# A written-out instruction order, replaced from about a sixth of the kernel onward

## The chip, the core and the metric

The kernel runs on one core of a Trainium2 chip. That core has five engines with instruction queues of their own: TensorE (PE in the profile, with PEld for its weight loads), VectorE (DVE), ScalarE (ACT), GpSimd (POOL) and SyncE (SP), which here only issues transfers. Each engine works through its queue strictly in order, and waits on semaphores where an instruction needs what another engine or a transfer has not yet delivered. The metric is the device time of one execution in microseconds; a smaller one is better.

## What is computed

Attention over 8 batches, 8 heads, 576 tokens and 64 dimensions a head, with 16 further "beacon" keys and values in front that every token may see, and then an ELU network over the 4608 tokens that result:

```python
scores = scale * q @ concat(beacon_k, k).T        # causal among the 576, beacons always seen
a = softmax(scores);  x = a @ concat(beacon_v, v) # per head; heads side by side: (4608, 512)
h = x @ w_in                                      # (4608, 2048)
g = where(h > 0, h, exp(min(h, 0)) - 1)
out = g @ w_out                                   # (4608, 512)
```

## The kernel before

**Attention.** Heads are taken in pairs: pair n is heads 2*(n%4) and 2*(n%4)+1 of batch n//4, 32 pairs in all. For batches 0 to 3 a pair's k and q are loaded (load_k, load_q), cast to bf16 (cast_pair, into one of three `sb` buffers), turned on PE (do_T) and copied out of PSUM (do_kT on DVE, do_qT on ACT or DVE). For batches 4 to 7 the loads are by token (load_tok, cast_tok) and the turning is done by transposing transfers on SP (turn_tok). The scores of a pair come in a few units SC (L568); ACT takes their exponential (L578, two instructions a unit, out of two PSUM banks into an `et` buffer), POOL zeroes what the causal mask hides (L583), PE multiplies by the values and a column of ones (AV, L597), and DVE divides (do_norm: L610 and L611). The result x is turned by PE or, from batch 2 on, by transposing transfers (turn_x, L617), into xT.

**The network.** It works on 11 tiles of tokens: two of 128, one of 256, then eight of 512 (tiles 3 to 10). In a tile of 512 the first matrix takes 16 steps of four matmuls (do_mm1, L649), each into one PSUM bank; here "step (p, i)" is step i of tile p. Each step's bank goes through three others: ACT takes exp into one of eight `wide` buffers (do_e, L656), a clamp to [0, 1] follows (do_clamp, L660), and DVE joins the two branches of ELU (do_join, L671), which frees the bank and the `wide` buffer and leaves half of a `gt` buffer. The second matrix of tiles 3 to 10 is done by the Strassen-Winograd scheme: seven products of half size (P1 to P7, do_PR, L725), each in two halves of eight matmuls, with DVE making four kinds of sums from the `gt` buffers (S3 L698, S1 L701, S2 L704, S4 L707). The sums of weights that it needs are made once (T1 to T4, tile `wt`); before that `wt` serves as further load buffers. Products leave PSUM by copies (do_Xcopy, ACT or DVE) and additions (do_Xadd, L735) into `wide` buffers, and those are written out by SP or ACT (do_put, L739). Tiles 0 to 2 use a plain second matrix (do_mm2, L767).

**What sets the order.** Nothing schedules at build time. All operations are first recorded with what they depend on and which buffers they take and give; each gets a number. Then Program.run walks three tables: ORDER (the numbers, in the order in which the operations are to be emitted, with -1 for a filler matmul), PICKS (a letter for every operation that more than one engine could do) and PLACES (which buffer of its kind each operation takes). Where two places of the list use the same buffer, the later one waits for the earlier. The lines that turn the tables into a program:

```python
for op in self.ops:
    if len(op.engines) > 1:
        op.eng = next(picks)
for i in order:
    ...
    for room in op.take:
        at = int(next(places), 36)
    ...
    op.fn(self.engines[op.eng], *got, *op.args)
```

An operation with a choice names its engines when it is recorded: the clamp is `add("GV", do_clamp, ...)`, so POOL or DVE; a cast of k and q is `"GA"`, POOL or ACT; a load or a put is `"SA"`, the queue of SP or of ACT. The join is DVE's alone, and exp is ACT's.

Of the kernel before, what the change touches and what calls it, by code (L numbers as in the profile page):

```python
# [29 lines left out]
301 251 254 261 278 302 320 958 279 303 280 282 288 304 281 1019 283 305 1020 309 306 311 959 284 308 340 1028  # L30
310 312 411 321 412 285 295 960 1065 322 323 428 1089 1033 1066 413 1067 1037 1090 512 1034 1035 1093 1038
1039 399 297 1094 1095 358 429 400 292 1057 1058 1059 1036 1049 1050 430 1051 409 324 1041 1091 1092 1042 1043
1040 1096 445 1068 462 446 307 414 1060 536 415 416 1081 1082 1083 410 359 1052 1097 290 1053 1054 463 313 417
431 432 433 1044 1029 1022 1023 1055 447 1024 434 341 342 1025 343 293 289 464 1056 344 1026 1084 1073 1074
1075 448 449 526 1085 1086 450 1076 407 465 1087 1045 1046 1047 1061 1062 314 1030 405 451 1063 466 1088 1048
1069 1070 1071 1072 408 1077 1078 1079 467 291 360 468 401 1064 649 978 979 1080 315 351 349 316 317 350 352
354 403 1098 980 981 1031 1101 1027 542 982 331 335 336 337 361 543 1102 362 332 334 1021 363 364 406 333 380
1099 381 1100 329 345 330 1105 508 1108 1106 371 365 346 1107 366 384 325 537 1109 1115 961 402 538 347 530
1104 372 531 983 385 506 374 368 375 326 328 353 1032 355 369 1103 1118 367 373 348 376 377 378 370 1112 544
379 327 1113 390 1120 382 392 1110 1111 1116 527 356 357 391 1121 383 520 539 540 541 386 387 521 522 1117 388  # L40
1126 1127 1142 393 395 389 397 418 479 480 481 1114 1128 1119 1124 419 1134 435 439 441 396 394 1135 1122 436
437 1130 404 1136 440 442 443 1125 424 444 425 514 1123 528 529 452 422 423 426 1131 427 515 504 453 454 1132
1152 1153 523 1160 484 510 485 458 475 476 1154 478 438 1161 1192 1193 1155 488 421 489 1156 1157 459 1162
1163 1158 1194 1195 627 505 524 532 1159 533 1184 1185 1186 1209 1168 1169 1170 1171 1176 1177 525 1138 1178
1148 1149 1144 1145 1150 1139 545 1187 1180 513 1181 1200 1201 643 644 1179 1146 1147 1151 1182 477 398 1183
1202 516 1137 1196 1197 1172 1198 1173 473 474 534 456 1164 1165 1174 460 1166 1208 617 1203 461 621 1204 1199
1188 517 518 457 622 1189 650 1190 469 1212 1175 1211 1167 492 496 1216 486 470 493 535 1141 455 1191 1213
1229 1217 1205 490 472 1210 1206 1207 1214 497 502 1215 1223 1224 1219 1220 420 482 471 494 501 487 1222 1221
500 495 483 1133 491 503 1218 1226 623 1227 1228 507 572 556 1231 573 628 1225 1230 1235 499 557 559 558 1237
637 638 576 552 498 553 550 551 1232 1241 577 1234 651 574 1233 1242 511 1243 519 645 1238 1239 1240 579 562  # L50
563 647 1252 560 586 1236 646 561 1263 1264 1271 1250 1287 587 578 1265 1266 1295 633 1272 1288 1299 1273 1274
1296 1297 1298 1300 1301 1267 1268 618 1245 509 593 740 652 554 629 630 1289 624 631 750 1269 594 1290 1251
648 1249 601 1270 1255 1256 588 1246 1247 565 1303 1304 602 1305 570 632 566 567 615 568 1311 1257 569 1302
1312 639 1313 555 1258 641 1253 1259 1260 1261 1291 1292 597 625 1306 1320 1275 640 1314 634 598 1262 1319 734
571 1276 591 582 546 1279 1293 1294 575 1283 583 580 564 584 592 635 756 547 548 599 1280 1281 581 1284 585
642 1277 1323 636 1278 600 595 1340 596 549 1324 589 613 603 590 606 1307 1315 1285 604 1282 1308 609 1327 607
608 1286 1316 1309 1317 1328 1310 1318 735 619 741 718 1331 611 1143 1329 673 674 679 659 660 680 1330 1341
1322 1326 1337 1334 1346 677 653 693 654 656 694 1321 1325 1335 678 1342 742 1332 1366 1367 863 751 682 757
1368 662 1248 616 728 1333 1345 1343 626 743 1344 661 736 1390 1338 1374 1375 620 758 744 745 1422 1378 1379
1391 1380 1392 1406 1369 1398 1399 737 1376 1377 1381 1400 1382 1393 1339 1431 681 1394 676 738 729 1370 1383  # L60
1363 1401 1423 1348 1424 1395 1396 1407 726 1426 722 1425 1371 1414 1140 752 1349 1408 847 754 1409 1386 1372
614 1384 1415 1416 1397 1360 1373 1336 1352 1353 1385 739 695 1417 1387 1388 1389 1354 655 1350 1427 612 730
1428 663 1361 1433 657 664 759 1402 1403 746 666 1404 1410 605 1411 1429 675 841 1405 665 706 1418 1419 1420
658 747 1244 731 707 748 732 749 1412 1413 1356 1357 1421 1358 753 669 683 670 1351 689 672 1430 1437 690 691
1451 696 704 697 1434 1438 1435 692 1364 1432 684 686 671 685 698 699 667 687 610 688 705 1436 1439 1444 668
1440 708 709 848 700 701 1129 1452 1456 702 710 703 790 766 791 767 711 733 713 714 827 857 724 1445 1446 1447
842 858 1457 864 865 755 1254 760 761 780 800 801 1441 1365 1453 1442 1454 1448 1443 1449 1450 792 723 1497
1498 802 1517 1455 1355 1347 781 1518 1519 1499 1481 1533 835 1493 1520 1494 1495 768 782 829 1482 725 1501
1534 849 1496 1500 851 1535 1536 852 866 717 1543 1459 720 836 1525 1526 1527 1528 1472 1485 1486 1487 1477
1478 716 1460 1461 1474 1479 783 1480 1362 762 727 1488 828 1529 1530 793 831 850 1531 1532 1513 1509 1467  # L70
1521 1502 769 1468 1510 1514 1503 1504 1522 1511 1515 1483 843 1505 1512 1489 1463 1506 1547 1484 830 719 1523
1524 1469 1490 1491 1541 1516 712 796 797 845 786 787 1464 844 833 1562 825 1492 1542 1546 774 764 765 1507
763 1537 798 859 721 1465 1549 1538 805 1545 789 1508 1539 1553 1540 811 1550 853 855 775 770 776 812 1475
1471 1551 806 777 1563 1544 1548 832 799 779 861 860 803 846 854 837 1552 1568 1556 1557 1554 1566 862 771 794
784 839 838 840 785 815 1565 788 804 1564 1559 1558 816 773 772 807 795 1555 715 813 808 814 1574 1567 820 778
817 818 809 810 821 1560 1561 1575 1458 1466 856 1585 1576 1577 873 874 819 887 893 888 1570 894 1571 1572 824
1573 907 867 908 909 1604 889 1620 868 1473 895 1621 1605 869 875 1606 1644 1645 1646 1607 1608 1588 1622 1589
870 1590 1591 1462 1636 1637 1609 1592 1593 1638 823 1639 1623 1612 1613 1616 890 1610 1611 1470 1594 1595
1647 896 1614 1596 1597 1598 1600 1601 1648 1649 1650 1578 1599 1617 1602 1615 877 871 876 878 1618 1579 1587
1619 1580 1624 826 872 1625 1586 1603 822 1651 1652 1628 1629 1630 891 892 897 1626 1640 1641 1569 1655 1631  # L80
1653 912 898 913 1632 1627 1633 834 1642 1634 1660 903 881 882 1656 920 1661 1643 1635 1657 1673 883 1583 904
905 884 901 899 1659 1654 900 906 886 885 1663 1359 1662 1666 1664 1674 910 1667 1476 1670 1675 921 1678 918
902 924 1658 1665 1677 911 879 925 922 880 914 1671 915 916 917 928 1672 923 1668 919 927 1681 1682 1676 931
1669 1685 1686 1683 1689 1690 1691 1679 1680 1692 1707 1743 1699 1687 1700 929 1703 1708 1709 930 926 1711
1739 1744 1712 1715 1731 1745 1713 1710 1701 1838 1702 1723 1740 1741 1714 1694 1582 1698 1759 1742 1764 1732
1697 1696 1584 1693 1716 1717 1704 1746 1718 1724 1725 1726 1581 1695 1760 1705 1706 1763 1755 1761 1756 1757
1733 1758 1762 1818 1819 1727 1728 1729 1730 1734 1766 1770 1719 1720 1751 1752 1753 1721 1722 1842 1765 1747
1748 1749 1750 1754 1834 1735 1835 1836 1820 1769 1736 1737 1858 1738 1768 1821 1771 1767 1837 1843 1850 1851
1772 1839 1773 1826 1775 1774 1810 1852 1811 1784 1684 1785 1827 1853 1828 1829 1822 1781 1790 1840 1777 1841
1776 1844 1823 1824 1825 1846 1875 1812 1787 1814 1815 1866 1782 1845 1813 1859 1860 1854 1778 1789 1867 1783  # L90
1792 1793 1805 1786 1804 1816 1868 1877 1817 1862 1855 1788 1847 1848 1849 1861 1830 1831 1856 1857 1779 1870
1882 1808 1863 1864 1832 1895 1874 1878 1879 1833 1876 1865 1871 1688 1780 1794 1796 1795 1886 1883 1884 1797
1800 1801 1802 1809 1885 1892 1880 1803 1869 1887 1872 1873 1881 1896 1791 1888 1900 1893 1889 1890 1891 1894
# [1005 lines left out]
```

## Time and profile before

| | us |
|---|---|
| median of 3 runs | 342.77 (339.97 to 343.51) |
| profiled execution, its own time | 343.58 |
| its span, first to last instruction | 341.7 |
| PE busy in the span | 328.6 (96%) |
| DVE busy | 265.4 (78%) |
| ACT busy | 227.4 (67%) |
| POOL busy | 178.6 (52%) |

The profiled execution is 0.81 us above the median, and 1.9 us of its own time lie outside the span. The profile gives busy times by engine, by slice of the span and by group of instructions, and for every idle stretch of an engine what ended it. A busy share is an average: what counts here are the stretches in which PE stands still. Durations of overlapping matmuls are longer than the distance from one to the next; the sums below use distances.

### The profile page before, as it was taken

The numbers are of one execution on the slowest core, as the hardware profiler recorded it, in microseconds if no ns is written. First come the engines' busy times: TensorE is split into PE (matmuls) and PEld (weight loads), VectorE is DVE, ScalarE is ACT, GpSimd is POOL, SyncE is SP. The second block draws the span as 40 slices with busy tenths as digits, with TensorE's granted clock in tenths as the row PEclk, the third lists the DMA queues.
The fourth block names the chain that finished last, engine by engine and source line by source line (L and its number), as shares of the span: only waits on it lengthen the run. The fifth ranks groups of instructions, "written<-read, shape, count | busy, mean of one in ns | idle before, by whom it ended". The sixth has DMA issues, their size and how long they took to land.

```text
span 341.7 us, 9661 instructions
## 1 busy us (share of the span) xinstructions
PE 328.6 (96%) x3712; PEld 230.8 (68%) x3712; DVE 265.4 (78%) x594; ACT 227.4 (67%) x446; POOL 178.6 (52%) x317
## 2 busy tenths in 40 slices
PE   8999999999989999999999999999999999999995
PEld 6677866545678546865688877457855696456784
DVE  4677784789996599859967998598829992998972
ACT  2797897786965875498687686579587733654320
POOL 3596988178793495257518652347256421442300
PEclk9999999999999999999999999999999999999998
DMA  7999999888785887588689975995781005100024
GB/s 215 240 249 228 217 265 229 225 220 161 204 193 114 177 163 156 105 189 133 132 159 182 185 148 128 246 179 98 89 234 43 33 14 126 57 1 0 33 94 153
DMA packets 131885, 51.42 MB, mean 150 GB/s; under 512 B 113408, under 2 KB 128256, under 8 KB 131840
## 3 DMA queue, kind: packets, MB, share of 16 engines
q1 hardware_dynamic: 122688, 41.80, 58.3%
q0 software_dynamic: 4224, 4.19, 7.5%
q10 hardware_dynamic: 4928, 4.82, 5.0%
q8 instruction: 29, 0.48, 0.6%
q14 instruction: 16, 0.13, 0.2%
HBM read 37.22 MB, written 9.44 MB: 137 GB/s over the span
## 4 chain that ended last, share of the span: by engine, by line
PE 62%; DVE 13%; POOL 8%; DMA 7%; issue 5%; ACT 3%; SPq 0%; ACTq 0%; DVEq 0%; POOLq 0%
PE bank L649 23%; PE bank L725 22%; DVE gt L671 7%; PE bank L597 6%; PE bank L568 5%; PE bank L767 3%; POOL et L583 3%; DMA w_in<-in_moe_w_in_dram 3%; DVE wide L660 3%; POOL wide L660 2%; POOL sb L351 2%; DMA out_dram<-wide 1%; DMA st<-in_q_dram 1%; ACT et L578 1%; DVE x L611 1%
## 5 line engine op out<-in xcount | busy, mean ns | idle before, releaser
L649 PE MATMUL bank<-xT,w_in 128*128 128x512 f16 (+2 forms) x768 | 133.4, 326 | 1.6 <-DVE gt L671 1.2
L578 ACT ACTIVATE et<-bank 128x512 f16<-128x512 f32 (+3 forms) x226 | 110.5, 579 | 27.5 <-PE bank L568 23.3
L671 DVE SCALAR_TENSOR_TENSOR gt<-wide,bank 128x512 f16<-128x512 f32 x144 | 94.9, 687 | 29.1 <-POOL wide L660 27.9
L656 ACT ACTIVATE wide<-bank 128x512 f32<-128x512 f32 x144 | 83.3, 607 | 43.7 <-PE bank L649 34.8
L649 PEld LDWEIGHTS <-w_in 128*128 128x128 f16 x768 | 68.0, 98 | 52.0 <-issue 2.1
L660 POOL TENSOR_SCALAR wide<-wide 128x512 f32<-128x512 f32 x100 | 63.1, 640 | 71.5 <-ACT wide L656 70.8
L583 POOL TENSOR_SCALAR_AFFINE_SELECT et<-et 128x256 f16<-128x256 f16 (+3 forms) x145 | 66.7, 479 | 53.7 <-ACT et L578 51.4
L725 PEld LDWEIGHTS <-gt 128*128 128x128 f16 x768 | 72.2, 98 | 16.4 <-issue 1.8
L725 PE MATMUL bank<-w_out,gt 128*128 128x256 f16 x512 | 63.7, 273 | 1.3 <-DVE gt L701 0.7
L597 PE MATMUL bank<-v,et 128*128 128x65 f16 (+1 forms) x960 | 37.8, 193 | 2.7 <-POOL v L351 0.9
L597 PEld LDWEIGHTS <-et 128*128 128x128 f16 (+1 forms) x960 | 35.3, 97 | 7.2 <-issue 2.9
L568 PE MATMUL bank<-qT,kT 64*128 64x80 bf16 (+4 forms) x744 | 35.2, 225 | 0.4 <-DVE gt L671 0.2
L351 POOL CAST sb<-st 128x1024 bf16<-128x1024 f32 (+6 forms) x28 | 26.7, 959 | 16.0 <-DMA st<-in_k_dram 5.9
L349 ACT ACTIVATE wide<-bank 128x512 f32<-128x512 f32 x24 | 14.4, 600 | 30.3 <-PE bank L725 29.7
L611 DVE TENSOR_TENSOR x<-bank,rl 128x256 f16<-128x256 f32 (+2 forms) x68 | 32.1, 471 | 2.3
L725 PE MATMUL bank<-wt,gt 128*128 128x256 f16 x256 | 32.3, 273 | 0.1
L568 PEld LDWEIGHTS <-kT 64*128 64x128 bf16 x744 | 20.5, 95 | 14.0 <-issue 10.6
L660 DVE TENSOR_SCALAR wide<-wide 128x512 f32<-128x512 f32 x44 | 23.6, 544 | 3.5 <-ACT wide L656 3.4
L735 DVE TENSOR_TENSOR wide<-bank,wide 128x512 f32<-128x512 f32 x24 | 16.2, 687 | 9.9 <-PE bank L725 8.5
L351 DVE COPY kT<-bank 128x16 bf16<-128x16 bf16 (+4 forms) x48 | 16.4, 449 | 6.1 <-PE bank L445 2.0
L610 DVE RECIPROCAL rl<-bank 128x4 f32<-128x4 f32 (+2 forms) x68 | 12.2, 180 | 9.8 <-PE bank L597 6.1
L698 DVE TENSOR_TENSOR ss<-gt 128x512 f16<-128x512 f16 x32 | 17.0, 534 | 0.6 <-PE bank L725 0.2
(60 smaller groups left out, 240.9 us busy)
## 6 DMA issues: line engine op xcount, KB each, us to landing
vst<-in_v_dram SPq DMA_DIRECT2D x23, 256.0 KB, 4.7
out_dram<-wide SPq DMA_DIRECT2D x22, 256.0 KB, 2.5
st<-in_q_dram SPq DMA_DIRECT2D x16, 256.0 KB, 4.3
out_dram<-wide ACTq DMA_DIRECT2D x14, 256.0 KB, 2.4
st<-in_k_dram SPq DMA_DIRECT2D x12, 256.0 KB, 3.8
st<-in_k_dram SPq DMA_DIRECT2D x8, 288.0 KB, 6.7
st<-in_q_dram SPq DMA_DIRECT2D x8, 288.0 KB, 8.0
w_in<-in_moe_w_in_dram POOLq DMA_DIRECT2D x4, 512.0 KB, 10.5
```

Of the source, the lines that this page charges most:

```text
L351: e.tensor_copy(out=out, in_=in_)
L568: e.matmul(out=banks[h][:, o:o + w], lhsT=kT[D * h:D * h + D, P * jc:P * jc + P], rhs=qT[D * h:D * h + D, q0:q0 + w], start=True, stop=Tru ...
L578: e.activation(out=et[:, h, 0:w], in_=scs[n, u][h][:, 0:w], func=AFT.Exp, bias=0.0, scale=float(1.0 / (D ** 0.5)))
L583: e.affine_select(out=part, in_=part, compare_op=ALU.is_ge, fill=fill0, base=q0 + NB - P * jc, pattern=[[0, 2], [0, times], [1, dw]], chan ...
L597: e.matmul(out=av[:, c:c + D + 1], lhsT=ets[tuple(unit)][0:m, h, col:col + P], rhs=v16s[b % 2][0:m, jc, 2 * hp + h, 0:D + 1], start=(jc == ...
L611: e.tensor_tensor(out=x16s[b % 2][:, blks[0]:blks[-1] + 1:step, P * hp:P * hp + P].rearrange("q i (h d) -> q i h d", d=D), in0=av[:, :, :, ...
L649: e.matmul(out=bank[:, o:o + z - a], lhsT=w_in16[:, cc, P * fc:P * fc + P], rhs=xTa[:, cc, a % RING:a % RING + z - a], start=(cc == 0), st ...
L656: e.activation(out=t, in_=hpss[p, i], func=AFT.Exp, bias=0.0, scale=1.0)
L660: e.tensor_scalar(out=t, in0=t, scalar1=1.0, scalar2=0.0, op0=ALU.min, op1=ALU.max)
L671: e.scalar_tensor_tensor(out=out, in0=in0, scalar=1.0, in1=in1, op0=ALU.subtract, op1=ALU.max)
L698: e.tensor_tensor(out=ss, in0=quarter(p, 0, 0, j), in1=quarter(p, 1, 0, j), op=ALU.subtract)
L725: e.matmul(out=bank[:, HC * s:HC * s + HC], lhsT=left[:, c, P * s:P * s + P], rhs=RIGHT[k][:, fc], start=(fc == 0 and s == 0 and k in HEAD ...
```

## The change

ORDER, PICKS and PLACES get other numbers from the 457th entry of the list on; the first 456 stay. Operations, their kinds, the dependences, and the numbers of buffers are the same. The order is one that was made for varying lengths of all operations off TensorE and for three paces of the transfers. The diff is tables only:

```diff
@@ -27,91 +27,91 @@
 976 236 264 977 241 259 238 265 255 260 1017 237 256 276 300 272 258 266 277 287 1018 267 273 257 252 253 294
-301 251 254 261 278 302 320 958 279 303 280 282 288 304 281 1019 283 305 1020 309 306 311 959 284 308 340 1028
+301 251 254 261 278 302 320 958 279 303 280 282 288 304 281 1019 283 305 1020 309 306 311 959 284 445 340 341
...
 PICKS = (
-    "GSGSVSGSVSVSAVVASSGVASGVASSGVSSGVSAGVSAVVSSVVAVAVVAVAAVVVASASGSGSASASSGASSGVSSGVSSGVAVAVGSASASGSASASSAASSGVSSG"
+    "GSGSVSGSVSVSAVVASSGVASGVASSGVSSGVSAGVSAVVSSVVAVAVVAVAAVVVASASGSGSASASSGASSGVSSGVSSGVAVAVGSGSGSASASASSAASSGVSSG"
...
```

Counted over the whole program, PE has the same instructions in another order. Eleven clamps go from DVE to POOL: DVE has 33 instead of 44, POOL 111 instead of 100. By tile, POOL has 11 instead of 13 in tile 3, then 12 (10), 13 (11), 11 (8), 11 (8), 12 (12), 12 (11) and 13 (11) in tiles 4 to 10, the number before in brackets. One copy of a product goes from DVE to ACT, two puts from SP's queue to ACT's, and a few casts change between POOL and ACT. The load buffers in `wt` stay in use for longer, and T3, which writes there first, comes later in DVE's queue.

Three places of the new order, as the built program has them. The first is POOL at the beginning of tile 3. `sb` rows are casts of a pair's k and q, `v` rows casts of values, and `wide` rows (L660) clamps. Before:

```order
L351 CAST sb_94<-wt 128x2x9x64
L351 CAST sb_92<-st_89 128x2x9x64
L660 TENSOR_SCALAR wide_112<-wide_112 128x512
L660 TENSOR_SCALAR wide_114<-wide_114 128x512
L660 TENSOR_SCALAR wide_115<-wide_115 128x512
L660 TENSOR_SCALAR wide_109<-wide_109 128x512
```

and now:

```order
L351 CAST sb_94<-wt 128x2x9x64
L351 CAST v_0_77<-vst_96 128x8x64
L660 TENSOR_SCALAR wide_111<-wide_111 128x512
L660 TENSOR_SCALAR wide_113<-wide_113 128x512
L351 CAST sb_92<-st_89 128x2x9x64
L660 TENSOR_SCALAR wide_114<-wide_114 128x512
```

The cast into sb_92 stood ahead of all of the tile's clamps on POOL, and now stands behind two of them. The clamps of steps (3, 1), (3, 4) and (3, 6), which POOL did, are now DVE's.

The second is DVE late in tile 4, from the join of step 11 to the sum S1 with which the second half of P5 begins (the last L701 row of each). Before:

```order
L671 SCALAR_TENSOR_TENSOR gt_123<-wide_111,bank_143 128x512
L701 TENSOR_TENSOR gt_122<-gt_122,gt_123 128x2x256
L698 TENSOR_TENSOR ss_131<-gt_119 128x512
L671 SCALAR_TENSOR_TENSOR gt_124<-wide_115,bank_139 128x512
L701 TENSOR_TENSOR gt_119<-gt_119,gt_120 128x2x256
L610 RECIPROCAL rl<-bank_142 128x6
L611 TENSOR_TENSOR x_1_80<-bank_142,rl 128x3x128
L701 TENSOR_TENSOR gt_118<-gt_118,gt_124 128x2x256
```

and now, from the join of step 13:

```order
L671 SCALAR_TENSOR_TENSOR gt_123<-wide_108,bank_137 128x512
L698 TENSOR_TENSOR ss_134<-gt_121 128x512
L704 TENSOR_TENSOR gt_122<-gt_122 128x2x256
L701 TENSOR_TENSOR gt_120<-gt_120,gt_119 128x2x256
L701 TENSOR_TENSOR gt_121<-gt_121,gt_123 128x2x256
L704 TENSOR_TENSOR gt_120<-gt_120 128x2x256
L704 TENSOR_TENSOR gt_121<-gt_121 128x2x256
L610 RECIPROCAL rl<-bank_143 128x6
L611 TENSOR_TENSOR x_1_80<-bank_143,rl 128x3x128
L671 SCALAR_TENSOR_TENSOR gt_125<-wide_114,bank_137 128x512
L698 TENSOR_TENSOR ss_131<-gt_117 128x512
L701 TENSOR_TENSOR gt_117<-gt_117,gt_125 128x2x256
```

PE used to take the halves of the products as P1, P2, P1, P5, P5; now it takes P1, P1, P2, P6, P5, P2, P6, P5, with step (4, 15) of the first matrix after the second P1, so that the second half of P5 stands three halves later among them.

The third is POOL in tile 7; `et` rows (L583) are masks. Before, the clamps of steps 9, 3 and 7:

```order
L660 TENSOR_SCALAR wide_112<-wide_112 128x512
L351 CAST v_0_77<-vst_96 128x8x64
L660 TENSOR_SCALAR wide_114<-wide_114 128x512
L660 TENSOR_SCALAR wide_109<-wide_109 128x512
L583 AFFINE_SELECT et_106<-et_106 128x2x112
L583 AFFINE_SELECT et_101<-et_101 128x2x128
L351 CAST sb_94<-st_89 128x1024
```

and now, the clamps of steps 14, 3, 15, 13, 11 and 5:

```order
L660 TENSOR_SCALAR wide_111<-wide_111 128x512
L660 TENSOR_SCALAR wide_109<-wide_109 128x512
L583 AFFINE_SELECT et_107<-et_107 128x2x512
L351 CAST sb_94<-st_89 128x1024
L660 TENSOR_SCALAR wide_108<-wide_108 128x512
L583 AFFINE_SELECT et_104<-et_104 128x2x80
L660 TENSOR_SCALAR wide_111<-wide_111 128x512
L583 AFFINE_SELECT et_104<-et_104 128x2x112
L660 TENSOR_SCALAR wide_109<-wide_109 128x512
L660 TENSOR_SCALAR wide_114<-wide_114 128x512
```

Six clamps of the tile now stand within ten rows of POOL, with a wide mask and a cast among them.

More of the change, by code (lines that the diff above doesn't have):

```diff
@@ L105 @@
     "71025610275621301020135613602153241753612212430357344612230574623166031447260054600132770510101322746125134742"
-    "03510264776355042422703243132450475656643175724210652740601216573471045341753005341370631511432077516245502134"
-    "0037130554164060327811123952A147B354C006602D1004713E3702261024715563340721121613475413210101655730642325600103"
-    "74225450610032453750662740522433147053256072360567722712136031453272061312406711334323545327200617234501511251"
-    "37260202182377304130652317400735226237711142612376411603724300165D32377B4C125400320103344625140713255171117021"
-    "403072465107223467240371355212110007465137040713564320134002254716151763394E431575513432B56130731A357215146673"
-    "0052157533746010215237030124645200463120473310652126043507112563530D420464084024101167A544210614E6152410621310"
-    "7432231307242047602541363061751324651274654135246546713214572764C17162713594477E225110055362424332167700245501"
-    "41301762415314506022064573026672326501573014833625B315072A317592214E460057053514416C520035142214D0074213361407"
-    "571202413462030403231602"
+    "03510264776355042422703243132450475656643175724210652740601216573471045341753005341370631511432077516523402413"
+    "150570035612024834674019A206B3170C212D5543143761E0520563401111260132575743410573445561342502465734016223363002"
+    "57041614122335716504017161014125737624557632144567652140170671422533141140463322564347603103244422617501073341"
+    "6542910523073234613216407034602024237312504237412123044711710046231705320451072366550B1773235641022A532E051610"
+    "2327143565770061825343547641763025601504331505663340212212560706147120132516C261D32223011465423772109264404353"
+    "115013162436122420434410157213306013640635703102214136577013610465B7314031E62060271134D25761606003121387402036"
+    "1163415750061573140033066323716102523711664274516425274631560327346A7031454745130730364675524107397C6604320125"
+    "1074760511324270613614352705613620701612753336244015B062753E63126850D537410324C6051502371673472366405704124450"
+    "722149141275A04030676270"
 )
```

6 lines of the change are left out of this document (3 added, 3 removed), and 130 rows, old and new, of the table ORDER.

## The prediction

> **What bounds the kernel now.** First the busy time by engine, in the stretch that the change leaves alone, the stretch that it reorders, and the tail (columns: length; then busy time and count of PE, PEld, DVE, ACT, POOL; PE's granted clock; transfers):
>
> ```profile
> 0.00:63.50 63.50, 59.44 (x862) 45.05 (x863) 42.41 (x135) 46.71 (x103) 44.39 (x90) 1.00 1.07 236
> 63.50:337.50 274.00, 269.15 (x2854) 185.78 (x2851) 223.03 (x459) 180.05 (x343) 134.17 (x228) 1.00 0.64 130
> 337.50:341.70 4.20, 0.05 (x1) 0.00 (x0) 0.00 (x0) 0.60 (x1) 0.00 (x0) 0.80 0.56 186
> ```
>
> PE is the bound, at full granted clock, and its work is the same after the change. Its idle time is 4.06 us up to 63.5 us, where PE's order is kept, 274.00 - 269.15 = 4.85 us in the reordered stretch, and 4.15 us after the last matmul. So an order can win about 4.85 us, 1.4%, and lose any amount.
>
> Next, what ended PE's waits from 63.5 us on (total, times, longest):
>
> ```profile
> PE bank L649 <- DVE gt L671: 1.2, 3, 0.8
> PE bank L597 <- POOL et L583: 0.9, 1, 0.9
> PE bank L725 <- DVE gt L701: 0.7, 1, 0.7
> PE bank L725 <- DVE gt L671: 0.7, 2, 0.4
> PE bank L767 <- DVE gt L671: 0.7, 1, 0.7
> ```
>
> No weight or input load is among them; DVE's joins and sums are, and one mask on POOL. The timeline has the five large ones (start, length, instruction, in brackets the idle time before it):
>
> ```profile
> 74.64 1.02 PE L767 MATMUL bank<-w_out,gt 128*128 128x512 f16 x4 [0.65 <-DVE gt L671]
> ...
> 101.26 1.09 PE L597 MATMUL bank<-v,et 128*128 128x65 f16 x30 [0.87 <-POOL et L583]
> ...
> 133.24 1.59 PE L725 MATMUL bank<-w_out,gt 128*128 128x256 f16 x13 [0.44 <-DVE gt L671]
> 136.97 0.83 PE L725 MATMUL bank<-w_out,gt 128*128 128x256 f16 x6 [0.68 <-DVE gt L701]
> ...
> 219.55 1.68 PE L649 MATMUL bank<-xT,w_in 128*128 128x512 f16 x7 [0.80 <-DVE gt L671]
> ```
>
> Together 3.44 of the 4.85 us; the other 1.41 us are small pieces.
>
> **Part by part.** PE's own pace, needed for every margin:
>
> ```profile
> 285.31 7.93 PE L649 MATMUL bank<-xT,w_in 128*128 128x512 f16 x36
> ...
> 335.64 1.91 PE L725 MATMUL bank<-wt,gt 128*128 128x256 f16 x16
> ```
>
> A step of the first matrix (4 matmuls) or half a product (8) is about 0.87 us of PE.
>
> *The wait at 74.64.* A plain second-matrix step waited for the bank of step (3, 4). What lay behind:
>
> ```profile
> 68.57 1.42 POOL L351 CAST sb<-st 128x1152 bf16<-128x1152 f32 x1 [4.03 <-PE bank L649]
> 69.97 2.34 POOL L660 TENSOR_SCALAR wide<-wide 128x512 f32<-128x512 f32 x4
> 70.61 2.50 DVE L671 SCALAR_TENSOR_TENSOR gt<-wide,bank 128x512 f16<-128x512 f32 x4 [0.90 <-POOL wide L660]
> 73.01 1.06 DVE L351 COPY kT<-bank 128x512 bf16<-128x512 bf16 x3
> ```
>
> POOL had waited 4.03 us for a cast, then the clamps came in a row, DVE lost 0.90 us, and the kT copy went ahead of the join. In the new order that PE step comes after eight first-matrix steps and one turning, about 7.5 us of PE after the turning of pair 10. Ahead of the join that it needs, DVE has two kT copies (2.1 us), a copy and a join-sized qT pair (0.7 and 1.1), one clamp (0.5) and three joins (2.1): 6.5 us. Margin 1.0 us, and the three early clamps no longer pass POOL. I take the 0.65 us as gone.
>
> *The waits at 133 and 137.* DVE was full there:
>
> ```profile
> 130.00:140.00 10.00, 8.88 (x139) 7.67 (x138) 9.76 (x24) 3.39 (x7) 3.78 (x7) 1.00 0.68 134
> ```
>
> The late one is the second half of P5, waiting for its S1. Now three more halves (2.6 us) stand ahead of it, and step (4, 15), the last one it needs, is 5 halves and three value products earlier, about 6 us; exp, clamp and join of that step and S3 and S1 take 0.6 + 0.6 + 0.7 + 0.4 + 0.4, and a norm of 0.7 stands between: margin about 2 us. The second half of P6, one place ahead, needs one sum more: about 0.8 us. I take both waits, 1.12 us, as gone.
>
> *The wait at 219.55.* It began on ACT:
>
> ```profile
> 212.74 0.90 ACTq L739 DMA_DIRECT2D out_dram<-wide  x2
> ...
> 217.71 1.65 ACT L656 ACTIVATE wide<-bank 128x512 f32<-128x512 f32 x3 [2.45 <-DMA out_dram<-wide]
> ```
>
> Two puts issued at 212.74 held `wide` buffers that the exps of tile 7 took some 3 us of PE later; ACT waited 2.45 us, until 4.9 us after the issue. Now two first-matrix exps of that tile take over put buffers 4.0 and 5.4 us of PE after the puts. A transfer as slow would cost ACT 0.9 us, against 2.45 us that cost PE 0.80. I take the 0.80 us as gone.
>
> *The wait at 101.26.* A value product waited for a mask behind a row of ten:
>
> ```profile
> 95.31 5.90 POOL L583 TENSOR_SCALAR_AFFINE_SELECT et<-et 128x224 f16<-128x224 f16 x10
> ...
> 128.43 1.08 ACT L578 ACTIVATE et<-bank 128x512 f16<-128x512 f32 x2
> 100.45 0.90 ACT L578 ACTIVATE et<-bank 128x400 f16<-128x400 f32 x2 [0.93 <-PE bank L597]
> ```
>
> In the new order POOL's masks are spread, but ACT has eleven pairs of exps (three at 1.08, eight near 0.9), one exp of 0.6, one product copy of 0.6 and a qT pair of 0.9 between the first scores of that group and the value product that takes the last one's bank: 12.5 to 12.8 us, against 12.6 us of PE. I keep 0.3 of the 0.87 us.
>
> *Clamps from DVE to POOL.* The mean of one on either engine, and the largest POOL groups beside them:
>
> ```profile
> L660 DVE TENSOR_SCALAR wide<-wide 128x512 f32<-128x512 f32 x44 | 23.6, 544 | 3.5 <-ACT wide L656 3.4
> ...
> L660 POOL TENSOR_SCALAR wide<-wide 128x512 f32<-128x512 f32 x100 | 63.1, 640 | 71.5 <-ACT wide L656 70.8 <-DVE gt L671 0.2
> L583 POOL TENSOR_SCALAR_AFFINE_SELECT et<-et 128x224 f16<-128x224 f16 x32 | 13.9, 437 | 14.2 <-ACT et L578 13.6 <-POOL sb L351 0.7
> L583 POOL TENSOR_SCALAR_AFFINE_SELECT et<-et 128x160 f16<-128x160 f16 x32 | 13.4, 422 | 8.1 <-ACT et L578 6.9 <-issue 1.2
> L351 POOL CAST sb<-st 128x1024 bf16<-128x1024 f32 x11 | 12.1, 1104 | 7.1 <-DMA st<-in_k_dram 5.9 <-DMA vst<-in_v_dram 1.2
> L583 POOL TENSOR_SCALAR_AFFINE_SELECT et<-et 128x1024 f16<-128x1024 f16 x5 | 5.6, 1129 | 13.3 <-ACT et L578 13.3
> L701 DVE TENSOR_TENSOR gt<-gt,gt x32: 410/459/1218, 89.3 to 327.5; 128x512 f16<-128x512 f16 x32
> ```
>
> DVE loses 11 x 0.544 = 6.0 us of its 223, POOL gains 11 x 0.640 = 7.0 us on 134. Neither is path by itself. But in tile 7 six clamps, two small masks, a wide mask and a cast now stand in a row: 6 x 0.640 + 0.437 + 0.422 + 1.129 + 1.104 = 6.93 us, with an exp (0.6) ahead and a join (0.7) behind 8.2 us. PE's work from the step that feeds the first clamp to the scores that want the last join's bank is four steps, four halves and some 1.6 us of attention, 8.6 us: a margin of 0.3 to 0.4 us. Tiles 4, 5, 6 and 10 have more clamps on POOL too. No row shows what such a row of clamps does to PE: at best nothing, at worst the last rival below. I take 1.0 us over five tiles, half the margin lost in each, nearer to nothing because POOL is busy 134 of 274 us there.
>
> The last row above has one S1 at 0.41 us at least and 1.22 at most. The Trainium skill (SBUF — State Buffer, "Who interferes with whom") says why that may be: a DVE instruction with two SBUF inputs and a GpSimd instruction that reads SBUF use one shared port pair, and the later one is blocked for the whole of the other. By that rule the clamps speak against the change: 7.0 us more of GpSimd work meets two-input DVE work, 64 us of the 341.7 by the four groups of sums, for an estimated 1.3 us on DVE. That is small beside the 6.0 us that DVE loses, so the sum stays.
>
> *The tail.* The last half of P4, a copy, a put: the same in both orders, 4.15 us. The remaining 1.41 us of small waits I leave as they are.
>
> The sum: -0.65 - 1.12 - 0.80 - 0.57 + 1.0 = -2.14 us. The profiled execution's own 343.58 us would become 341.4; it lies 0.81 us above the median of 342.77, so the forecast is 342.77 - 2.14 = **340.6 us**.
>
> **The rivals.**
>
> *Nearly all of the idle time goes.* The masks and puts are spread and DVE is 6 us lighter, so every wait in the reordered stretch can fall: 342.77 - 4.85 = 337.9 us, up to 339.3. Against it: several margins are 0.3 us, and one DVE sum can be 0.8 us longer than another.
>
> *The waits only move.* The old order also had its steps lined up and lost 4.85 us to lengths that differed from place to place; the new one has the same eight banks and eight `wide` buffers. Then 342.8 us, the change doing nothing that it says.
>
> *POOL becomes the late engine, and the kernel is slower.* If POOL's steps stretch by a quarter where clamps stand in rows, tile 7's 6.93 us become 8.66, 1.73 us more against 0.3 of margin: 1.4 us, and as much in tiles 4, 5, 6 and 10, 7.2 us in all. With the recovered 3.14 us that is 342.77 + 4.1 = 346.8 us. It decides from a stretch of about 4% at tile 7. For it: the clamp's mean on POOL, 0.640 us, has collisions in it already. Against it: POOL waits for ACT for 70.8 us before its clamps.
>
> **How the numbers follow.** The forecast's case (339.3 to 342.0) has 0.45, nearly all gone 0.23, moved waits 0.16, late POOL 0.16. About 1%, 3.43 us, is what a measurement of this kernel can tell from no change: faster means under 339.3, slower over 346.2. Faster is the second case and a share of the first: 0.30. Slower is most of the last: 0.15 with 0.02 from unnamed trouble, 0.17. The rest, 0.53, is within 1%. The range leaves out the upper end of the late POOL and the lower end of the second case, about 0.1 each: 337.9 to 345.6 us.
>
> **What would show it.** Right: PE's idle time between its 63rd microsecond and the tail falls to about 2.7 us, no PE wait at the plain second matrix in tile 3 nor at P5 of tile 4, no ACT wait for a put over 1 us in tile 7. DVE's busy time falls by some 5 to 6 us, POOL's rises by 7. The POOL rival: PE waits for joins that waited for clamps, in tiles 4 to 7. Moved waits: the same sum under other names. Wrong for all: a wait for a load or a transposing transfer of over 1 us, since no row of before has one there.

## The result and the profile after

The changed kernel takes 337.84 us (median of 11 runs, 335.62 to 340.62) against 342.09 us (median of 11 runs of the kernel before): 0.9876 of it, with a 95% interval of 0.9837 to 0.9914. It is faster by 4.25 us. (Ratios compare the fast runs alone: a run more than 1.5% above the fastest of its kernel counts in the medians but not in them.) The forecast was 340.6 us, and the measured time lies 0.06 us below the range's lower end, in the reach of the rival in which nearly all idle goes.

First the busy time by engine up to the point where the orders part, and from there to PE's last matmuls, in the new kernel's profile (columns as in the prediction: length; PE, PEld, DVE, ACT, POOL with counts; granted clock; transfers):

```profile
0.00:61.30 61.30, 58.30 (x862) 44.55 (x863) 42.88 (x135) 46.55 (x103) 45.99 (x90) 1.00 1.06 238
61.30:329.50 268.20, 266.40 (x2854) 186.45 (x2851) 213.91 (x447) 182.00 (x344) 137.43 (x238) 1.00 0.66 134
```

Its span is 333.8 us against 341.7, so this pair of profiles shows 7.9 us. Of these 2.2 us lie ahead of the first changed PE instruction (63.5 against 61.3 us; with fillers counted, the orders part at the 468th entry of the list and not at the 457th). The reordered stretch, with the same 2,854 matmuls, is 274.00 - 268.20 = 5.80 us shorter. PE's idle time in it falls from 4.85 to 1.80 us, and PE's busy time falls as well, from 269.15 to 266.40 us, although its work is the same.

What PE still waits for, in the same view as before (total, times, longest):

```profile
PE bank L649 <- DMA xT<-x: 0.7, 1, 0.7
PE bank L597 <- POOL et L583: 0.6, 1, 0.6
PE bank L597 <- DVE gt L671: 0.2, 1, 0.2
```

The rows of the named waits are gone, at 74, 101, 133, 137 and 219 us alike, and two new ones stand early: at 96.5 us in tile 3, and at 110.0 us at the first matmul of tile 4. The clamps, by engine (count; then minimum, median and longest in ns):

```profile
L660 POOL TENSOR_SCALAR wide<-wide x111: 604/612/902, 28.5 to 313.7; 128x512 f32<-128x512 f32 x111
L660 DVE TENSOR_SCALAR wide<-wide x33: 411/427/1169, 65.9 to 317.1; 128x512 f32<-128x512 f32 x33
```

One profile is one execution. So both kernels were profiled once more, and further runs took the change apart.

### The profile page after: what moved, and what is told of

It reads as the page before. It is cut to its first block, busy times and chain, and to the rows that moved or that the text cites. A ratio compares the mean times of both kernels' runs of the same rounds, so it can differ in the third digit from the quotient of the medians.

```text
span 333.8 us, 9671 instructions
## 1 busy us (share of the span) xinstructions
PE 324.8 (97%) x3712; PEld 231.0 (69%) x3712; DVE 256.8 (77%) x582; ACT 229.1 (69%) x447; POOL 183.4 (55%) x328
## 4 chain that ended last, share of the span: by engine, by line
PE 78%; DMA 7%; POOL 6%; DVE 4%; issue 2%; ACT 2%; SPq 0%; POOLq 0%; DVEq 0%
PE bank L649 30%; PE bank L725 26%; PE bank L597 8%; PE bank L568 6%; PE bank L767 3%; PE bank L354 3%; DMA w_in<-in_moe_w_in_dram 3%; POOL et L583 3%; POOL wide L660 2%; DMA out_dram<-wide 1%; DMA xT<-x 1%; ACT et L578 1%; DMA qT<-sb 1%; PE bank L444 1%; DVE gt L671 1%
## 5 line engine op out<-in xcount | busy, mean ns | idle before, releaser
L656 ACT ACTIVATE wide<-bank 128x512 f32<-128x512 f32 x144 | 84.3, 607 | 43.5 <-PE bank L649 35.5
L660 POOL TENSOR_SCALAR wide<-wide 128x512 f32<-128x512 f32 x111 | 68.9, 628 | 68.8 <-ACT wide L656 66.3
L671 DVE SCALAR_TENSOR_TENSOR gt<-wide,bank 128x512 f16<-128x512 f32 x144 | 93.8, 686 | 16.5 <-POOL wide L660 15.3
L583 POOL TENSOR_SCALAR_AFFINE_SELECT et<-et 128x256 f16<-128x256 f16 (+3 forms) x145 | 66.1, 475 | 50.9 <-ACT et L578 38.3
L725 PE MATMUL bank<-w_out,gt 128*128 128x256 f16 x512 | 62.7, 273 | 0.0
L568 PE MATMUL bank<-qT,kT 64*128 64x80 bf16 (+4 forms) x744 | 34.0, 225 | 0.3
L349 ACT ACTIVATE wide<-bank 128x512 f32<-128x512 f32 x25 | 14.8, 599 | 26.1 <-PE bank L725 25.8
L568 PEld LDWEIGHTS <-kT 64*128 64x128 bf16 x744 | 20.7, 95 | 12.4 <-issue 9.2
L351 POOL CAST sb<-st 128x1024 bf16<-128x1024 f32 (+6 forms) x28 | 25.5, 912 | 5.0 <-DMA st<-in_q_dram 5.0
L660 DVE TENSOR_SCALAR wide<-wide 128x512 f32<-128x512 f32 x33 | 17.0, 516 | 14.0 <-ACT wide L656 13.7
```

The lines of the kernel that those rows point to most:

```text
L351: e.tensor_copy(out=out, in_=in_)
L568: e.matmul(out=banks[h][:, o:o + w], lhsT=kT[D * h:D * h + D, P * jc:P * jc + P], rhs=qT[D * h:D * h + D, q0:q0 + w], start=True, stop=Tru ...
L583: e.affine_select(out=part, in_=part, compare_op=ALU.is_ge, fill=fill0, base=q0 + NB - P * jc, pattern=[[0, 2], [0, times], [1, dw]], chan ...
L656: e.activation(out=t, in_=hpss[p, i], func=AFT.Exp, bias=0.0, scale=1.0)
L660: e.tensor_scalar(out=t, in0=t, scalar1=1.0, scalar2=0.0, op0=ALU.min, op1=ALU.max)
L671: e.scalar_tensor_tensor(out=out, in0=in0, scalar=1.0, in1=in1, op0=ALU.subtract, op1=ALU.max)
```

## The experiments

### Both kernels once more

Nothing is edited; each kernel is run and profiled a second time. For the kernel before:

> The kernel before once more, for a second profile. The two profiles shown differ by 2.20 us (63.52 against 61.32) at the PE instruction up to which both orders are the same. If that is chance of one execution (theory: chance), this profile reaches that instruction somewhere between 61 and 64 us, and the rest of PE's work, 273.76 us before and 267.96 us after, is near 273. If the later orders reach back through loads that SP issues early (rival), it is at 63.5 again within 0.4 us. Its ratio to before should be 1.00 within its interval, about 0.004.

For the changed kernel:

> The changed kernel once more, for a second profile. Chance: the common first part ends anywhere between 61 and 64 us. Rival: at 61.3 within 0.4 us. Either way the reordered part should last near 268 us if the gain of 5.8 us there belongs to the order; if it was partly a lucky execution, 269 to 270, which is what the medians (4.25 us) would need. Time 336 to 340 us.

Measured: the kernel before 341.21 us (10 runs, 1.0001 of it, 0.9964 to 1.0037), the changed kernel 337.45 us (4 runs, 0.9858, 0.9802 to 0.9914). Their reordered stretches, of the old order and of the new:

```profile
62.00:335.30 273.30, 269.25 (x2854) 185.75 (x2851) 223.15 (x459) 180.05 (x343) 134.36 (x228) 1.00 0.63 132
```

```profile
62.40:332.10 269.70, 267.04 (x2854) 186.63 (x2851) 215.76 (x447) 182.18 (x344) 136.69 (x238) 1.00 0.63 134
```

The point where the orders part is reached at 62.0 us by the old and 62.4 us by the new kernel, so the 2.2 us of the first pair are chance. The reordered stretch is 273.65 us on average before and 268.95 after: **4.70 us** less, which agrees with the medians. Of these 4.70 us, 2.22 are idle time (4.85 and 4.05 before, 1.80 and 2.66 after) and 2.48 are busy time.

What PE waited for in the second execution of the old order, the five largest:

```profile
PE bank L597 <- POOL et L583: 0.9, 1, 0.9
PE bank L767 <- DVE gt L671: 0.8, 1, 0.8
PE bank L725 <- DVE gt L671: 0.7, 2, 0.5
PE bank L649 <- DVE gt L671: 0.4, 2, 0.2
PE bank L725 <- DVE gt L704: 0.3, 1, 0.3
```

Three of the five named waits are there again. The wait for S1 in tile 4 (0.68 us) and the one at tile 7's first matrix (0.80 us) are not (near the first of them, 38 matmuls later, PE waited 0.3 us for an S2). Two of the five terms of the sum were thus read from events that the same program need not have.

A measure that counts a wait in full is the distance from one matmul's start to the next. The table sums how much later than PE's pace matmuls start, for all those over 0.1 us late, worked out from the starts of PE's matmuls. Stretches are cut at equal PE work, at about the times of the new order's profile.

| stretch, about | before, twice | after, twice | change of the mean | predicted |
|---|---|---|---|---|
| 61 to 111 us (tile 3) | 2.60, 2.74 | 1.90, 2.97 | -0.24 | -1.22 |
| to 147 us (tile 4) | 1.96, 1.73 | 0.10, 0.37 | -1.61 | -1.12 |
| to 205 us (tiles 5 and 6) | 1.46, 1.23 | 0.26, 0.19 | -1.12 | 0 |
| to 232 us (tile 7) | 1.21, 0.43 | 0.78, 0.76 | -0.05 | -0.80 |
| to the tail (tiles 8 to 10) | 0.77, 0.79 | 0.00, 0.00 | -0.78 | 0 |
| sum | 8.00, 6.92 | 3.04, 4.29 | -3.80 | -3.14 |

The gain comes from places that are partly other than those named. The other 0.9 us of the 4.70 are differences under 0.1 us each.

### Half of one order, half of the other

```diff
-ORDER, PICKS, PLACES of one kernel
+the first 1020 entries of one kernel's order, then the operations left over in the other's order;
+a buffer that is taken at the join is replaced by a free one; one or two loads come later there;
+the filler matmuls of the first part all use one bank
```

New order first:

> The new order to the end of tile 4's products (about 147 us), from there the old order and the old engines. By the places that the prediction named, the waits at 74, 101, 133 and 137 us go and that at 219 stays: start to start they are 0.82 + 1.04 + 0.60 + 0.85 = 3.3 us, so 342.1 - 3.3 + 0.7 for the mask wait that is left, near 339.5 us. If what helps is DVE's relief by clamps in tiles 5 to 7 (rival), little of the gain shows here: about 341.5. If waits only move, the old part takes back what the first part wins: 342.

Old order first:

> The old order to the same amount of work (about 154 us), from there the new one. By the named places only the wait at 219 us (0.96 us start to start) goes, and a share of the small ones: 342.1 - 1.5 = 340.6 us. If the relief of DVE in tiles 5 to 7 matters most: 338.5 to 339. The two hybrids' gains should add up to the whole, 4.25 us; if they add up to clearly less, the two parts need each other.

Measured: 348.0 us (1.0142, 1.0098 to 1.0186) and 349.22 us (1.019, 1.014 to 1.024). Neither theory has this: both hybrids are slower than either kernel. The new order first, and then the old order first, PE's largest waits from 55 us on:

```profile
PE bank L649 <- DVE gt L671: 5.6, 4, 2.6
PE bank L649 <- ACT et L578: 0.6, 1, 0.6
```

```profile
PE bank L597 <- POOL et L583: 2.5, 2, 1.5
PE bank L597 <- DVE x L611: 2.0, 2, 1.5
PE bank L649 <- DVE gt L671: 1.2, 2, 1.0
```

By the measure of the table, 5.6 and 9.3 us are lost in the stretch with the join (147 to 205 us), where the leftovers of one order stand against the other's. Away from the join the halves behave as in their own kernels: tile 4 loses 0.00 us in the new half and 1.73 in the old, tiles 8 to 10 lose 0.89 in the old half and 0.00 in the new. So the totals say nothing on the shares of the gain. The stretches bear out the table in tile 4 and in tiles 8 to 10; tiles 5 to 7 they cannot test. The old half of the first hybrid also lost 5.0 us at tile 7, where ACT waited for two puts to land:

```profile
219.40 1.57 ACT L656 ACTIVATE wide<-bank 128x512 f32<-128x512 f32 x3 [3.67 <-DMA out_dram<-wide]
```

With 2.45 us of this wait PE stood 0.80 us in the first profile of before; with 1.45 and 1.18 us, one after the other, it did not stand in the second; with 3.67 us it stood 2.63 us. The hazard that the prediction named is real, and its size differed in each of these three executions.

### Clamps back to DVE in the new order

```diff
 engine of the clamps (4,3) (4,13) (5,10) (5,11) (6,5) (6,10) (6,11) (7,5) (7,8) (7,11) (9,6) (10,1) (10,5)
-POOL
+DVE
```

> The new order with 13 clamps put back from POOL to DVE, 2 to 3 in each of tiles 4 to 7, 1 in tile 9 and 2 in tile 10; nothing else. The prediction's account (the clamps cost PE 1.0 us on POOL and DVE's load is no path): 337.8 - 1.0 = 336.8 us. Rival, DVE's relief carries the gain: 13 x 0.544 = 7.1 us come back on DVE, of which a third to a half reaches PE, so 340 to 341 us with waits for joins in tiles 4 to 7. If neither engine is near its limit there: 337.8 within 0.8.

Measured: 339.29 us, 0.9906 of before (0.9864 to 0.9947), 1.4 us above the changed kernel's median, with intervals that overlap. In the profile the reordered stretch is 270.6 us, above both executions of the changed kernel, and the lost starts are 1.46 us in tiles 5 and 6 (0.26 and 0.19) and 1.56 in tile 7 (0.78 and 0.76), on joins:

```profile
PE bank L568 <- DVE gt L671: 1.6, 4, 0.9
```

The 336.8 us of the prediction's account lie below the interval (0.9864 of the 342.15 us that before took beside this run is 337.5), so these clamps do not cost 1.0 us on POOL. In this one profile DVE's relief is worth about 2.0 us of such waits in tiles 5 to 7.

### The same clamps to POOL in the old order

```diff
 engine of the same 13 clamps
-DVE
+POOL
```

> The old order with the same 13 clamps moved from DVE to POOL. By the prediction's account: POOL late by 1.0 us in an order that was not made for it, no gain: 343. By DVE's relief: DVE loses 13 x 0.544 = 7.1 us, POOL gains 8.3 us, PE's waits for joins and sums shrink by 1 to 2 us: 340 to 341. If the engine alone matters little and the order is what counts: 342 within 1.

Measured: 346.76 us, 1.0148 of before (1.0089 to 1.0206): slower by more than any theory had. To see whether it was the load or one place, the 13 were divided:

> The old order with only the two clamps of tile 4 of the 13 moved to POOL. The 13 together cost 4.6 us, and their profile has one place that accounts for most of it: a DVE clamp that took 3.25 us (0.42 at least) beside a gapless row of POOL clamps, masks and casts, a PE wait of 2.21 us for the join behind it, and then granted clock 0.5 for 3 us. If one collision is the cause (theory): 342.1 + 4, near 346, with that clamp over 2.5 us again and the granted clock near 0.5 after it. If the load on POOL is the cause (rival), 2 of 13 clamps cost 0.7: 342.8, and no clock below 0.9.

> The other 11 of the 13 clamps moved to POOL, in tiles 5 to 7, 9 and 10, in the old order. One collision as the cause: without it these clamps take 6.0 us off DVE and PE loses nothing for POOL: 341 to 342. Load on POOL as the cause: 11/13 of 4.6 us, near 346.

Measured: the two clamps of tile 4 alone 346.01 us, 1.0087 (1.0048 to 1.0126); the other eleven 342.37 us, 1.0007 (0.9973 to 1.0042). Two clamps thus cost about 3.0 us by the ratio, most of what all 13 cost, and one collision causes it. The eleven show one thing more: in the old order they relieve DVE by 3.0 us in the reordered stretch (223.1 to 220.15), half of the 6.0 expected, and that is worth nothing that can be measured. By the measure of the table that profile loses about 2.5 us in tiles 5 and 6, more than the 1.46 and 1.23 of before. In the profile with two clamps moved, first DVE and then POOL in tile 4 (start, length, instruction, in brackets the idle time before it):

```profile
122.84 3.25 DVE L660 TENSOR_SCALAR wide<-wide 128x512 f32<-128x512 f32 x1
126.13 1.88 DVE L671 SCALAR_TENSOR_TENSOR gt<-wide,bank 128x512 f16<-128x512 f32 x3
```

```profile
119.60 2.56 POOL L660 TENSOR_SCALAR wide<-wide 128x512 f32<-128x512 f32 x4
122.11 0.60 POOL L351 CAST v<-vst 80x512 f16<-80x512 f32 x1
122.69 0.61 POOL L660 TENSOR_SCALAR wide<-wide 128x512 f32<-128x512 f32 x1
123.25 0.41 POOL L583 TENSOR_SCALAR_AFFINE_SELECT et<-et 128x256 f16<-128x256 f16 x1
123.65 0.61 POOL L660 TENSOR_SCALAR wide<-wide 128x512 f32<-128x512 f32 x1
124.21 1.03 POOL L351 CAST sb<-st 128x1024 bf16<-128x1024 f32 x1
125.21 0.61 POOL L660 TENSOR_SCALAR wide<-wide 128x512 f32<-128x512 f32 x1
127.59 0.61 POOL L660 TENSOR_SCALAR wide<-wide 128x512 f32<-128x512 f32 x1 [1.77 <-ACT wide L656]
```

POOL works without a gap until 125.81 us, and the DVE clamp ends at 126.09 us: it stood for the rest of the row. In the old order as it was, the same clamp on DVE, and POOL's clamp and mask beside it:

```profile
124.29 0.61 DVE L660 TENSOR_SCALAR wide<-wide 128x512 f32<-128x512 f32 x1
```

```profile
124.00 0.61 POOL L660 TENSOR_SCALAR wide<-wide 128x512 f32<-128x512 f32 x1 [0.41 <-ACT wide L656]
124.57 0.60 POOL L583 TENSOR_SCALAR_AFFINE_SELECT et<-et 128x256 f16<-128x256 f16 x1
```

There POOL's row has a gap of 0.41 us, which the two clamps now fill, and the DVE clamp takes 0.61 us. But it meets the row behind that gap, and from 124.00 to 127.88 us POOL has no other: it passed between two POOL instructions, and the mask took 0.60 us in place of 0.41. So a missing gap alone does not explain the 3.25 us. With the two clamps moved, PE waited for the join behind the blocked clamp, and ran at half the granted clock afterwards (PE's rows, then busy times in two stretches):

```profile
126.87 0.28 PE L568 MATMUL bank<-qT,kT 64*128 64x256 bf16 x1 [2.21 <-DVE gt L671]
128.07 4.35 PE L649 MATMUL bank<-xT,w_in 128*128 128x512 f16 x12 [0.22 <-DVE gt L671]
```

```profile
124.60:128.10 3.50, 0.75 (x7) 0.32 (x6) 3.46 (x5) 1.19 (x3) 1.73 (x3) 1.00 1.00 196
...
129.20:131.80 2.60, 2.60 (x8) 0.91 (x6) 2.50 (x5) 1.50 (x3) 1.05 (x2) 0.50 0.99 182
```

By starts, the three waits cost 2.37 + 0.49 + 0.38 = 3.24 us, and seven matmuls behind them 6 x 0.213 + 0.353 = 1.63 us more. The third wait (0.22 us of idle time) stands in the old order as well.

### More clamps to POOL in the new order

```diff
 engine of the 17 clamps of tiles 4 to 7 that are DVE's
-DVE
+POOL
```

> The new order with all clamps of tiles 4 to 7 on POOL: 17 more, 17 x 0.640 = 10.9 us. A test of how near POOL is to being late, and of whether clamps block DVE's sums. If the margins are as thin as the prediction put them (0.3 to 0.4 us in tile 7, a stretch of 4% decides): each of the 5 more clamps of tile 7 is paid in full less 0.4 us, and about half of the rest: 337.8 + 2.8 + 3.8, near 344 us, PE waiting for joins that waited for clamps. If POOL has room, since it waits for exps most of the time: 337.8 to 339. The longest of DVE's sums should stay beside casts and rows of masks (1.0 to 2.7 us so far) and not appear beside the clamps, which a sum has to wait out one at a time (0.6 us).

Measured: 339.32 us, 0.9921 (0.9897 to 0.9946): 1.5 us more than the changed kernel, not 6. PE's largest waits from 60 us on:

```profile
PE bank L649 <- DMA xT<-x: 1.3, 1, 1.3
PE bank L568 <- DVE x L611: 1.1, 1, 1.1
PE bank L568 <- DVE gt L671: 0.6, 1, 0.6
```

The first is a transposing transfer, the second stands in tile 3, where nothing was edited. The waits for joins in tiles 4 to 7, all of them, come to 2.1 us by starts, against 1.04 and 0.95 us in the changed kernel's two profiles: 17 clamps more cost about 1.1 us. DVE's longest sum does stand beside a cast and a row of masks, as expected (2.68 us in tile 3), but one of 1.23 us at 157 us stands beside a cast and two clamps. So POOL had room. Why, POOL's rows in tile 7 of the changed kernel show:

```profile
215.00 1.36 POOL L660 TENSOR_SCALAR wide<-wide 128x512 f32<-128x512 f32 x2
216.32 0.39 POOL L583 TENSOR_SCALAR_AFFINE_SELECT et<-et 128x224 f16<-128x224 f16 x1
217.27 0.61 POOL L660 TENSOR_SCALAR wide<-wide 128x512 f32<-128x512 f32 x1 [0.56 <-ACT wide L656]
217.84 0.34 POOL L583 TENSOR_SCALAR_AFFINE_SELECT et<-et 128x160 f16<-128x160 f16 x1
218.13 0.61 POOL L351 CAST sb<-st 80x512 bf16<-80x512 f32 x1
219.56 1.19 POOL L660 TENSOR_SCALAR wide<-wide 128x512 f32<-128x512 f32 x2 [0.82 <-ACT wide L656]
```

POOL catches up with ACT and waits for exps between its clamps. The rows that stand together in the order do not stand together in time.

### Moving the sums out of the way in tile 3

In each of the two profiles of the changed kernel one sum S2 of tile 3 was stretched beside a row of masks, and not the same one. The two sums in the first execution, and the first of them in the second:

```profile
96.14 0.60 DVE L704 TENSOR_TENSOR gt<-gt 128x512 f16<-128x512 f16 x1
...
97.81 1.53 DVE L704 TENSOR_TENSOR gt<-gt 128x512 f16<-128x512 f16 x1
```

```profile
97.49 2.68 DVE L704 TENSOR_TENSOR gt<-gt 128x512 f16<-128x512 f16 x1
```

The first edit moves the waited-for mask and four sums (five operations in all):

```diff
 POOL
+L583 AFFINE_SELECT et_101<-et_101 128x2x112
 L583 AFFINE_SELECT et_104<-et_104 128x2x112
 L583 AFFINE_SELECT et_103<-et_103 128x2x128
-L583 AFFINE_SELECT et_101<-et_101 128x2x112
 DVE
-L707 TENSOR_TENSOR gt_126<-gt_126,gt_124 128x2x256
 L704 TENSOR_TENSOR gt_125<-gt_125 128x2x256
+L704 TENSOR_TENSOR gt_127<-gt_127 128x2x256
...
-L704 TENSOR_TENSOR gt_127<-gt_127 128x2x256
```

> The new order with PE's, ACT's and SP's rows as they are and six operations moved: on POOL the mask that PE waited for at 96.53 us goes ahead of two others; on DVE two sums S2 of tile 3 go ahead of the row of six POOL masks that stretched one of them to 1.54 us in one execution and 2.68 us in the other (0.41 at least), and two sums S4 behind it. If POOL's rows block DVE's sums, no S2 is over 0.9 us there, PE's wait for the mask (0.57 and 0.28 us) goes, and so does the 1.11 us that the second execution lost behind the 2.68 us: 337.2, a gain of 0.4 to 1.5 us that the profile shows between 94 and 102 us and that the time can hardly tell from none. If the stretch belongs to the sum itself, S2 stays over 1.2 us at its new place.

Measured: 338.55 us, 0.9893 (0.9859 to 0.9927), not to be told from the changed kernel. The mask wait is gone, but the sums ran into the row. DVE, POOL and PE:

```profile
96.98 3.23 DVE L704 TENSOR_TENSOR gt<-gt 128x512 f16<-128x512 f16 x2
```

```profile
97.30 0.78 POOL L351 CAST sb<-st 80x512 bf16<-80x512 f32 x1
98.04 2.38 POOL L583 TENSOR_SCALAR_AFFINE_SELECT et<-et 128x256 f16<-128x256 f16 x6
```

```profile
100.82 0.38 PE L568 MATMUL bank<-qT,kT 64*128 64x256 bf16 x5 [1.56 <-DVE x L611]
```

The first sum took 0.63 us and the second 2.68; they end at 100.21 us, with the row (it ends at 100.42). Behind the 1.56 us wait PE's granted clock was 0.50 for 3.4 us:

```profile
101.60:105.00 3.40, 3.40 (x43) 2.68 (x38) 1.46 (x6) 1.70 (x4) 1.36 (x2) 0.50 0.44 97
```

This does not yet separate the row from the sum itself. The next edit keeps this and puts a gap into POOL's row:

```diff
 POOL, behind the mask et_103 of the edit above
+L583 AFFINE_SELECT et_101<-et_101 128x2x80
 ...
 L351 CAST sb_92<-st_89 80x512
 ...
-L583 AFFINE_SELECT et_101<-et_101 128x2x80
```

The mask that now comes first waits for an exp; two of the row's five other masks come ahead of the cast, three behind it.

> The kernel with six operations moved, and now also POOL's row broken: the mask that waits for the last exp of that group (ACT ends it near 98.2 us) goes ahead of the cast and the other masks, so that POOL stands still for about 0.9 us where the two sums S2 fall. If a gapless row is what keeps the sum out, S2 takes 0.4 to 0.7 us each (3.23 us for both before this edit), and PE's 1.56 us wait behind them goes; 336.5 to 337.5 us. If the sum is slow for another reason, S2 stays over 1.2 us and the wait stays.

Measured: 338.34 us, 0.9894 (0.9856 to 0.9931). DVE and POOL:

```profile
98.38 1.16 DVE L704 TENSOR_TENSOR gt<-gt 128x512 f16<-128x512 f16 x2
```

```profile
95.69 3.58 POOL L583 TENSOR_SCALAR_AFFINE_SELECT et<-et 128x256 f16<-128x256 f16 x5 [0.18 <-ACT et L578]
100.03 1.07 POOL L583 TENSOR_SCALAR_AFFINE_SELECT et<-et 128x160 f16<-128x160 f16 x3 [0.76 <-ACT et L578]
```

With POOL's row changed the same two sums take 1.16 us instead of 3.23, and no PE wait stands between 94 and 102 us. So the stretch belongs to POOL's row and not to the sum. That the gap is what let the sums in is not shown: the first of them ended at 98.99 us, while POOL worked on without a gap until 99.27, and the edit also moved the cast out of the sums' way. The time is not better: in that execution PE lost 1.04 us at 78 us for a cast ahead of the edit, 0.78 us at 105 us for a copy, and 1.17 us at 113 us for a transposing transfer. No version here is measurably faster than the changed kernel.

## Why the prediction was wrong, by its steps

**The ceiling.** "An order can win about 4.85 us" took PE's idle rows for all there was to win. The mean gain in the stretch was 4.70 us, of which only 2.22 were idle. The reason can be read from the page's group of half products in the changed kernel (busy, mean ns of one):

```profile
L725 PE MATMUL bank<-w_out,gt 128*128 128x256 f16 x512 | 62.7, 273 | 0.0
```

A matmul is recorded as 273 ns long, while sixteen in a row take 1.91 us, 0.109 us apart. A late matmul therefore shows an idle time 0.16 us shorter than what it costs. Before, 21 and 19 matmuls started over 0.1 us late, after it 8 and 10. Eleven fewer are 1.8 us of PE's "busy" time that the prediction held fixed; the other 0.7 us of it are not accounted for. Idle time did fall to 1.80 and 2.66 us, near the forecast 2.7, and still was half of the gain.

**The waits at 74 and 101 us (-0.65, -0.57).** Both rows went, as argued. In the same stretch others took their place: another mask (0.57 us), a transposing transfer (0.7, at the first matmul of tile 4), or a norm behind a blocked sum (1.11). The rival of moved waits was right in this stretch alone: -0.24 us.

**The waits at 133 and 137 us (-1.12).** The step was right and somewhat small: 1.61 us.

**The wait at 219 us (-0.80).** The mechanism was right and the size was not: the old order's second execution lost nothing at that place. The forecast 0.9 us of ACT's wait for a put in the new order was 1.45 and 1.39 us, and its sign "no wait over 1 us" did not come true. Worth here: 0.05 us.

**"The remaining 1.41 us of small waits I leave as they are."** This step failed most. Tiles 5, 6 and 8 to 10 gave 1.90 us by starts, in pieces of 0.1 to 0.4 us, most of them waits for joins. DVE's relief bears on those, but only together with the new order: with 13 clamps put back, 1.46 us are lost again in tiles 5 and 6, while the old order gained nothing from the same relief by eleven clamps. How much the order gives without the clamps was not isolated: the hybrids lost more at their joins than there was to divide.

**Clamps on POOL (+1.0).** No such cost showed: with 13 clamps put back the median rose by 1.4 us, where the term called for a fall of 1.0 (17 more on POOL, too, cost 1.5 us by the medians). The margin of 0.3 us in tile 7 came from adding up a row of the order as if POOL were never to wait within it. That POOL waits 70 us for exps before its clamps was quoted against the rival and left out of this term.

**DVE's busy time.** Forecast 5 to 6 us less, measured 9.1 and 7.4 (223.03 and 223.15 to 213.91 and 215.76). POOL's was to rise by 7 and rose by 3.3 and 2.3 in the stretch. The Trainium skill's rule (SBUF — State Buffer, "Who interferes with whom"), weighed as speaking against the change, did not show as a cost: the time by which DVE's instructions in the reordered stretch exceed the tenth percentile of their kind fell from 20.8 and 20.7 us to 16.7 and 18.7. A clamp on DVE can be blocked by POOL too, and eleven of them went.

**The late POOL.** As a queue it did not occur in either order. As a block of DVE by POOL's row it did: two clamps in the wrong place made the old order 3 us slower.

**The chances.** Without the clamp term the sum was -3.14 us, and with the 1.41 us of small waits -4.55, near the 4.25 measured. That is the rival that nearly all idle goes, which had 0.23. Its number came near by luck: half of the idle time stayed (2.23 of 4.45 us on average), and the rest of the gain is time that shows as PE's work. By starts the named places gave 1.90 us of the 3.14 forecast, and the places that were put at nothing gave another 1.90.

## What to carry over

Count what an order can win by the starts of matmuls against their pace, not by idle time, and take two executions before a wait becomes a term: two of five here were not there the second time. A move of work between two engines that block each other is priced by place, not by load: eleven clamps cost nothing measurable, two others 3 us. Parts of two good orders, put together, were worse than either.

## What was not expected of the hardware

**A row on POOL can block DVE to its end.** A DVE clamp or sum that meets a POOL row does not always wait for one instruction: at worst it stood for all that was left of a gapless row, 3.25 us for a clamp (0.42 at least) and 2.68 us for a sum (0.41 at least). That is rare. In the thirteen profiles 1,069 clamps and sums on DVE overlap POOL's work; 28 of them stood while at least one whole POOL instruction passed, and eight, at two places of the kernel, while three or more did. The Trainium skill (SBUF — State Buffer, "Who interferes with whom") says that whoever issues first holds the shared ports for the whole instruction, and counts tensor_scalar, the clamp's kind, among those that can take them. The traces agree with this, and the eight show that the next POOL instruction can take them again ahead of the waiting DVE. The 1.53 us in the changed kernel's first execution are one of the eight: that sum met the same row later, and stood until its last mask too. What decides between passing and standing was not tested.

**Behind waits of 1.5 to 2.6 us PE's clock halved for 3.4 us.** The granted clock was 0.50 from 129.05 us with the two clamps of tile 4 moved (behind waits of 2.21 and 0.32 us) and from 129.03 us with all 13, from 222.27 us in the first hybrid (2.63 us) and from 169.49 us in the second (1.51 and 0.99 us), and from 101.59 us in the first edit of tile 3 (1.56 us), each time for 3.4 us. Behind single waits of 1.0 to 1.5 us in other runs it stayed at 1.00, and so it did behind one of 1.86 us at 159.5 us in the first hybrid. So the length of the one wait does not decide it, and what does was not tested. The Trainium skill (TensorE: Matmul & The Clock Gate, "Part 1: The HAM clock gate") gives an idle window of about 3.4 us; here PE was not idle that long: it worked for 0.75 us of the 3.5 us up to 128.1 us with the two clamps moved, and for 1.82 of the 3.6 us up to 101.6 us in the first edit of tile 3.
